# Two buffers for later units' queries, keys and values, six stage tiles, and a plan with other numbers

## The chip, the cores and the metric

The kernel runs on one core of one Trainium2 chip. The metric is device time in microseconds (us) of one launch. Before the change three runs took 918.61, 918.62 and 922.46 us, median 918.62. The engines are named as in the profile: PE is TensorE (matmuls; PEld its weight loads), DVE is VectorE, ACT is ScalarE, POOL is GpSimd, SP is SyncE, which issues all DMAs here, in order.

## What is computed

Windowed attention for 8 batches of 8 heads, 576 positions and 64 columns (heads 4 to 7 look at every fourth position), and then a two-layer network with a rational function between the layers, on 4608 tokens:

```python
scores = scale * np.matmul(q, k.transpose(0, 1, 3, 2))
mask_plain = (rel >= 0) & (rel < 32)
mask_dil = (rel >= 0) & (rel < 128) & (rel % 4 == 0)
attn = softmax(np.where(mask, scores, -1e9))
x = np.matmul(attn, v)          # to (tokens, 512)
h = x @ w_in                    # (4608, 512) x (512, 2048)
P = a[0] + a[1]*h + a[2]*h**2 + a[3]*h**3
Q = 1.0 + abs(b[0])*abs(h) + abs(b[1])*h**2
out = (P / (Q + 1e-6)) @ w_out  # (4608, 2048) x (2048, 512)
```

All is float32. The two large products are each made of three matmuls on a high and a low half of their operands.

## The kernel before

**Units.** The attention is cut into 48 units, six for each batch. A unit loads its queries and keys in one DMA (`qk`, 448 KB) and its values in another (`v`, 384 KB). PE makes its scores, DVE, ACT and POOL the softmax, and PE the product with the values. Units 0 to 5 (batch 0) turn their probabilities on PE. For units 6 to 47 DVE turns them in blocks into a stage tile `u`; a DMA stores that into `turned`, and two DMAs read it back as `pT`. After the values product DVE turns the result into another stage tile `y`, which goes through `results` and comes back as `z` in four DMAs; ACT and DVE or POOL then split `z` into `xh` and `xl`, the high and low half of the input of the network. Six units of a batch fill one chunk of 512 tokens. What of a batch lies beyond 512 tokens is stored to `left` and makes up a ninth chunk.

**Tiles.** The network runs over 144 tiles, one for a chunk and one of 16 column blocks of `w_in`. Tile i has a first product `h` (12 matmuls into one PSUM bank of two), an elementwise chain over DVE, ACT and POOL, and 12 matmuls of the second product into four PSUM banks. The chain ends with a row `a<-a,h` on DVE, which frees the PSUM bank: `h` of tile i + 2 waits for that row of tile i. Tiles 0 to 7 are of chunk 0, tiles 8 to 23 of chunk 1, tiles 24 to 31 the rest of chunk 0, and tiles 32 to 47 of chunk 2. So the first product of tile 8 also needs `xh` and `xl` of units 6 to 11. Chunk 2 takes the `x` slot of chunk 1, so its splits come after tile 23.

**Weights.** 32 weight blocks arrive as 64-bit numbers (512 KB each), and are joined to float32 in a stage tile (`wi_f`, `wo_f` on DVE) and split into two halves on ACT, DVE or POOL, all of it beside the units of chunks 0 and 1 and the first tiles.

**The order.** The class `Plan` writes the order of every engine's instructions before anything is built: a list scheduler with a cost for each operation, a time for each DMA (`DMA_NS`, `DMA_RATE`), a hop between engines, and for each tile pool its number of buffers (`plan.takes`). Among operations that could start, the rank decides, and ranks come from the tables `DUE` (when a batch's units are due, counted in tiles), `LATE` and `SLACK`. The engines then run their rows strictly in that order: a row that waits holds all that stand behind it. SP too issues in order, so a load that waits for its buffer holds the stores and reloads behind it.

`qk` and `v` of units 6 to 47 have one buffer each, in the pool `att`: the load of unit 7's values waits until unit 6's values product is done. The pool tag `stage` has 8 tiles, used in turn for `u`, `y`, `z`, weights in conversion, output copies and others. A unit's values product and the scores of the unit two later are one operation of the plan (`DEPTH`), so in PE's order they stand together.

Of the kernel before, what the change touches and what calls it, by code (L numbers as in the profile page):

```python
# [8 lines left out]
F32 = mybir.dt.float32  # L9
# [10 lines left out]
P = 128  # L20
# [7 lines left out]

START_S, START_O = ["A", "att"] * 3, ["B", "B", "B", "A", "B", "A"]
KIND = [0, 0, 0, 0, 1, 0]  # L30
DUE = [(-23.06, 3.81), (79.36, 5.81), (328.16, 47.85), (161.48, -7.11), (443.73, -17.31), (297.23, -16.95), (114.62, -18.15), (542.56, 10.22)]

LATE = {"ab": -240.26, "ql": -279.92, "pl": -62.25, "qq": -87.68, "t1": 0.97, "t2": -88.2, "ln": 264.97, "ex": -508.74, "g0": -102.98, "g1": -175.35, "g2": -162.43, "gh": -184.66, "gl": 248.86, "out": 3.92}
SLACK = {"sc": 2.61, "qk0": -23.4, "v0": -24.42, "load": -21.21, "wi": 7.7, "wo": -0.04, "w": -8.09, "gl": -0.92, "out": 0.87}

EARLY_TILES, BOTH_TILES = 36, 36

DEPTH, STAGE, AHEAD, ON_PE = 2, 8, 6, 2
LEFT = S - 512
RQ, RKEY, NV = 4 * 3 * 32, 4 * 128, 3 * 2 * 2 * 64  # L40
LOG_SHIFT = 40
# [36 lines left out]
class Plan:  # L78
# [3 lines left out]
    HOP = {"PE": 200.0, "ACT": 135.0, "DVE": 120.0, "POOL": 80.0, "SP": 0.0}  # L82
    MORE = {("PE", "ACT"): 40.0, ("ACT", "POOL"): 110.0, ("DVE", "POOL"): 110.0, ("DVE", "ACT"): 60.0, ("ACT", "DVE"): 15.0}
    DUE_HOP, WINDOW = 150.0, 200.0
    DMA_START, DMA_NS, DMA_RATE = 3300.0, 1600.0, 400.0
    PERIOD, PE_LATE = 4743.0, 105.0

    def __init__(self):
# [2 lines left out]
    def op(self, engs, rank, fn, *deps, dma=0, lock=False):  # L91
        o = Op(engs, rank, fn, deps, dma, lock)
        self.ops.append(o)
        return o
# [88 lines left out]
def tile_attention_moe(  # L183
# [16 lines left out]
    att = ctx.enter_context(tc.tile_pool(name="att", bufs=1))  # L200
# [3 lines left out]
    plan = Plan()  # L204
    op = plan.op
# [50 lines left out]
    class Unit:  # L256
# [4 lines left out]
            self.s, self.o_ps = two_banks(self.s_tag), two_banks(self.o_tag)  # L261

        def load_qk(self, pool, tag):
            t = pool.tile([P, RQ + RKEY], F32, tag=tag, name=f"qk{self.n}")
            load(t, qk[self.n])
            self.q = t[:, :RQ].rearrange("p (g i c) -> p g i c", g=4, i=3)
            self.k = t[:, RQ:].rearrange("p (g k) -> p g k", g=4)

        def load_v(self, pool, tag):
            self.v = pool.tile([P, NV], F32, tag=tag, name=f"v{self.n}")  # L270
            load(self.v, vp[self.n])

        def scores(self):
# [205 lines left out]
        def plan(self, by, tags):  # L479

            b, u, start = self.b, self.u, self.start
            (qp, qt), (vpool, self.vt) = tags if start else ((att, "qk"), (att, "v"))
            self.by = by
            lq = op({"SP": 430}, 0, lambda e: self.load_qk(qp, qt), dma=(RQ + RKEY) * 512)
            self.lv = lv = op({"SP": 430}, 0, lambda e: self.load_v(vpool, self.vt), dma=NV * 512)
            prev, clear = None, []
            masks = [masked, identity] if self.on_pe else []
            if len(Unit.open) >= DEPTH:
                prev = Unit.open.pop(0)
            if prev:  # L490
                sc = op({"PE": 1320 + 300 * self.on_pe}, 0, lambda e: (prev.av(), self.scores()), *prev.placed, prev.lv, lq, *masks)
                clear = prev.finish(sc)
            else:
                sc = op({"PE": 1000 + 300 * self.on_pe}, 0, lambda e: self.scores(), lq, *masks)
            if self.on_pe:
                ma = sc
            else:
                ma = op({"DVE": 400 + 70 * len(MASK_AT[u])}, 0, lambda e: self.mask(), sc, masked)
            if start and KIND[u]:
                mx = op({"DVE": 660}, 0, lambda e: self.max_bank(), ma)  # L500
                su = ex = sm = op({"ACT": 1850}, 0, lambda e: self.exp_bank(), mx)
            else:
                mx = op({"DVE": 470}, 0, lambda e: self.max(), ma)
                su = op({"DVE": 500}, 0, lambda e: self.sub(), mx)
                ex = op({"ACT": 425}, 0, lambda e: self.exp(), su)
                sm = op({"DVE": 470}, 0, lambda e: self.sum(), ex)
            rc = op({"DVE": 300}, 0, lambda e: self.recip(), sm)
            no = op({"POOL": 790}, 0, lambda e: self.norm(e), rc)
            if start:
                tr = op({"PE": 550}, 0, lambda e: self.transposes(), no, identity)  # L510
                pl = op(BOTH, 0, lambda e: self.place(e), tr)
                plan.takes(tr, "h", 2, [pl])
                self.placed = [pl]
            else:
                tr = op({"DVE": 580}, 0, lambda e: self.turn(), no)
                pu = op({"SP": 430}, 0, lambda e: self.put(), tr, dma=P * 384 * 4)
                mv = op({"SP": 900}, 0, lambda e: self.move(), pu, dma=P * 384 * 4 + 160000)
                pu.slack = 0.0
                plan.takes(tr, "stage", STAGE, [pu])
                self.placed = [mv]  # L520


            if not start:
                sc.follows.append(Unit.last_read[0])
            Unit.last_read = [Unit.last_read[1], tr if start else su]
            for o, before in zip((lq, lv, sc), Unit.last):
                if before not in o.follows:
                    o.follows.append(before)
            Unit.last = (lq, lv, sc)
            (first_loads if start else unit_loads).extend((lq, lv))  # L530
            if start:
                early.extend((lq, lv))
            for o in (sc, ma, mx, su, ex, sm, rc, no, tr, *self.placed):
                o.slack = 0.0
            sc.slack = SLACK["sc"]
            lq.slack = SLACK["qk0" if start else "load"]
            lv.slack = SLACK["v0" if start else "load"]
            plan.takes(lq, qt, 1, [sc])
            plan.takes(sc, self.s_tag, 1, [su, *clear])
            plan.takes(su, "p", 2, [tr])  # L540
            plan.takes(mx, "mx", 2, [su])
            plan.takes(sm, "sm", 2, [no])
            if start:
                av = op({"PE": 1000}, 0, lambda e: self.av(), *self.placed, lv)
                av.slack = 0.0
                self.finish(av)
            else:
                Unit.open.append(self)

        def finish(self, av):  # L550
            b, start = self.b, self.start
            main, left = self.pieces()
            got = av
            if not start:
                to = op({"DVE": 590}, 0, lambda e: self.turn_out(), av)
                po = op({"SP": 430}, 0, lambda e: self.put_out(), to, dma=P * 384 * 4)
                got = op({"SP": 1800}, 0, lambda e: self.move_out(), po, dma=P * 384 * 4 + 160000)
                to.slack = po.slack = got.slack = 0.0
                plan.takes(to, "stage", STAGE, [po])
            eh = op({"ACT": sum(172 + 2 * c[1] / 1.4 * 0.75 for c, _ in main)}, 0, lambda e: self.evac_hi(), got)  # L560
            low = {"DVE": sum(120 + 2 * c[1] / 0.96 for c, _ in (main + left if start else main))}
            if not start:
                low["POOL"] = sum(100 + 2 * c[1] / 0.49 for c, _ in main)
            el = op(low, 0, lambda e: self.evac_lo(e), eh, lock=not start)
            eh.slack = el.slack = 0.0
            el.by = self.by
            lf = None
            if left:
                lf = op({"SP": 430 * len(left)}, self.by + 2.0, lambda e: self.put_left(), el if start else got, dma=P * 2 * LEFT * 4 + 60000)
                left_done.append(lf)  # L570
                if start:
                    plan.takes(el, "stage", STAGE, [lf])
            if start:
                plan.takes(self.placed[0], "a", 2, [av])
                plan.takes(av, self.o_tag, 1, [el])
            else:
                plan.takes(got, "stage", STAGE, [x for x in (el, lf) if x])
                plan.takes(self.placed[0], *(("p", 2) if self.n % 2 else ("pT", 1)), [av])
            plan.takes(self.lv, self.vt, 1, [av])
            if b not in x_done:  # L580
                x_done[b] = []
                plan.takes(eh, "x" + x_slot(b), 1, h_done[b])
            else:
                eh.deps.append(x_done[b][0])
            x_done[b] += [eh, el]
            return [el] if start else [to]
# [267 lines left out]
    identity = op({"POOL": 1000}, -89, lambda e: make_idents())  # L854
# [13 lines left out]
    for b in range(1, B):  # L868
        last, step = DUE[b]
        for u in range(NU):  # L870
# [124 lines left out]
```

## Time and profile before

| | |
|---|---|
| three runs, median | 918.62 us |
| the profiled execution | 921.15 us |
| its span, first to last instruction | 919.4 us |
| mean granted clock of PE | 0.989 |
| DMA | 105.81 MB, 115 GB/s over the span |
| most DMA issues | qk x48 (448 KB), v x48 (384 KB), weights x32 (512 KB), pT x84 (96 KB) |

The span's slices on the page give each engine's busy share, PE's granted clock and the DMA engines' share. Idle time of an engine counts only where it holds the chain that ends last; on the page 67% of that chain is PE's. The critical rows are shown where the prediction uses them.

### The profile page before, as it was taken

Reading aid. Unit: us, or ns where it says so; the run is one execution under the profiler, and the core shown is the slowest. Engines: PE = TensorE matmul, PEld = TensorE weight load, DVE = VectorE, ACT = ScalarE, POOL = GpSimd, SP = SyncE. Lnnn points to the kernel's source line nnn. Section 1 sums busy time; section 2 is a strip of 40 time slices with the busy share of each in tenths; the row PEclk is TensorE's granted clock in tenths of the full one; section 3 lists DMA queues with packets and bytes.
Section 4 is the critical chain, followed back from the end, with each engine's and each line's share of the span. In section 5 each row is a group of like instructions: output and inputs, shape, how many; then the busy total and the mean of one; then the engine's idle time right before and its main releaser. Section 6 shows DMA issues by size and latency. Waiting matters only on the chain.

```text
span 919.4 us, 21111 instructions
## 1 busy us (share of the span) xinstructions
PE 880.5 (96%) x8106; PEld 712.5 (77%) x8106; DVE 744.3 (81%) x1322; ACT 677.9 (74%) x1082; POOL 482.9 (53%) x419
## 2 busy tenths in 40 slices
PE   6858899999999999999999999999999999999998
PEld 4646688777888888788878888887888878888876
DVE  4787898999988988888879878987879777657656
ACT  3666899777767877777777777767777688777764
POOL 2456657475545664456455555545455444544442
PEclk9979999999999999999999999999999999999999
DMA  9668543335553343434343334422233220001001
GB/s 343 202 216 267 181 149 115 129 102 176 165 176 103 111 142 116 129 100 128 90 155 112 102 92 145 148 65 83 100 121 98 77 69 1 1 0 47 1 1 46
DMA packets 90372, 105.81 MB, mean 115 GB/s; under 512 B 40736, under 2 KB 67744, under 8 KB 90272
## 3 DMA queue, kind: packets, MB, share of 16 engines
q1 hardware_dynamic: 90272, 104.47, 35.6%
q8 instruction: 63, 1.03, 0.5%
q14 instruction: 37, 0.30, 0.1%
HBM read 76.39 MB, written 28.05 MB: 114 GB/s over the span
## 4 chain that ended last, share of the span: by engine, by line
PE 67%; DVE 11%; DMA 7%; ACT 7%; issue 3%; POOL 3%; SPq 2%; POOLq 0%; ACTq 0%; DVEq 0%
PE h L211 30%; PE out L211 30%; PE pair L211 4%; ACT r L214 4%; DVE a L220 3%; DVE h L220 3%; SPq L208 2%; POOL a L223 2%; DMA results<-y 2%; DMA turned<-u 1%; DMA qk<-in_qk_dram 1%; DMA z<-results 1%; DVE t L217 1%; DMA v<-in_vp_dram 1%; DMA wi_raw<-in_w_in_dram 1%
## 5 line engine op out<-in xcount | busy, mean ns | idle before, releaser
L211 PE MATMUL h<-xh,wi 128*128 128x512 f32 x1136 | 379.6, 396 | 10.3 <-DVE a L220 10.1
L211 PE MATMUL out<-gh,wo 128*128 128x512 f32 x1136 | 355.5, 394 | 0.0
L223 POOL TENSOR_TENSOR a<-r,a 128x512 f32<-128x512 f32 x126 | 163.1, 1295 | 256.0 <-ACT r L214 241.1
L211 PEld LDWEIGHTS h<-xh,wi 128*128 128x128 f32 x1136 | 215.9, 190 | 63.1 <-DVE a L220 17.4
L211 PEld LDWEIGHTS out<-gh,wo 128*128 128x128 f32 x1136 | 211.4, 189 | 45.7
L223 POOL TENSOR_TENSOR gl<-a,gh 128x512 fp32r<-128x512 f32 x135 | 186.8, 1383 | 72.0 <-ACT gh L214 56.4
L211 PE MATMUL h<-xl,wi 128*128 128x512 f32 x568 | 223.6, 394 | 0.0
L211 PE MATMUL out<-gl,wo 128*128 128x512 f32 x568 | 221.9, 391 | 0.9 <-DVE gl L217 0.9
L220 DVE SCALAR_TENSOR_TENSOR a<-a,r 128x512 f32<-128x512 f32 x141 | 100.2, 710 | 100.5 <-ACT r L214 98.7
L214 ACT ACTIVATE r<-a,ln_bias 128x512 f32<-128x512 f32 x141 | 101.8, 722 | 90.9 <-POOL a L223 87.3
L214 ACT ACTIVATE r<-a,ab_t 128x512 f32<-128x512 f32 x141 | 115.0, 815 | 15.0 <-DVE a L220 6.4
L211 PEld LDWEIGHTS out<-gl,wo 128*128 128x128 f32 x568 | 107.0, 188 | 24.0 <-DVE gl L217 1.3
L211 PEld LDWEIGHTS h<-xl,wi 128*128 128x128 f32 x568 | 108.0, 190 | 21.7
L214 ACT ACTIVATE t<-h,na_t 128x512 f32<-128x512 f32 x142 | 109.6, 772 | 11.5 <-PE h L211 11.5
L214 ACT ACTIVATE a<-h 128x512 f32<-128x512 f32 x140 | 83.4, 596 | 41.4 <-PE h L211 37.8
L220 DVE SCALAR_TENSOR_TENSOR h<-h,na_t,r 128x512 f32<-128x512 f32 x142 | 106.6, 751 | 7.0 <-ACT r L214 6.1
L220 DVE SCALAR_TENSOR_TENSOR h<-t,na_t,h 128x512 f32<-128x512 f32 x142 | 107.2, 755 | 4.8
L214 ACT ACTIVATE r<-r,exp_bias 128x512 f32<-128x512 f32 x144 | 104.3, 724 | 4.6
L217 DVE TENSOR_TENSOR t<-t,h 128x512 f32<-128x512 f32 x142 | 96.3, 678 | 11.2 <-ACT t L214 8.9
L220 DVE SCALAR_TENSOR_TENSOR a<-a,h 128x512 f32<-128x512 f32 x140 | 96.2, 687 | 4.6
L214 ACT ACTIVATE gh<-a 128x512 fp32r<-128x512 f32 x133 | 83.4, 627 | 18.9 <-PE out L211 14.7
L223 POOL TENSOR_TENSOR p<-p,sm 128x384 f32<-128x384 f32 x48 | 45.3, 945 | 39.8 <-DVE sm L342 35.1
(105 smaller groups left out, 691.4 us busy)
## 6 DMA issues: line engine op xcount, KB each, us to landing
qk<-in_qk_dram SPq DMA_DIRECT2D x48, 448.0 KB, 4.8
v<-in_vp_dram SPq DMA_DIRECT2D x48, 384.0 KB, 3.9
out_dram<-os SPq DMA_DIRECT2D x36, 256.0 KB, 2.3
wi_raw<-in_w_in_dram SPq DMA_DIRECT2D x16, 512.0 KB, 5.3
wo_raw<-in_w_out_dram SPq DMA_DIRECT2D x16, 512.0 KB, 6.2
turned<-u SPq DMA_DIRECT2D x42, 192.0 KB, 2.2
pT<-turned SPq DMA_DIRECT2D x84, 96.0 KB, 2.5
results<-y SPq DMA_DIRECT2D x42, 192.0 KB, 2.5
```

The lines of the kernel that those rows point to most:

```text
L208: pin(nc.sync.dma_start(dst, src))
L211: pin(nc.tensor.matmul(o, lhs, rhs, start=start, stop=stop))
L214: pin(nc.scalar.activation(o, i, func, **kw))
L217: pin(nc.vector.tensor_tensor(o, x, y, op))
L220: pin(nc.vector.scalar_tensor_tensor(o, x, s, y, op0, op1))
L223: pin(nc.gpsimd.tensor_tensor(o, x, y, op))
```

## The change

It gives `qk` and `v` of units 6 to 47 two buffers each, cuts the stage tiles from 8 to 6, gives the leftover stores a rank 20 tiles after their unit's due time instead of 2, and changes numbers that only the planner reads: the tables of due times and ranks, a DMA's time and rate, and the PE times of units 0 to 11. No instruction's arithmetic changes.

```diff
-DUE = [(-23.06, 3.81), (79.36, 5.81), ...
-LATE = {"ab": -240.26, "ql": -279.92, ...
-SLACK = {"sc": 2.61, "qk0": -23.4, "v0": -24.42, "load": -21.21, ...
+DUE = [(-24.06, 4.46), (-57.85, 3.6), ...
+LATE = {"ab": -115.18, "ql": -320.79, ...
+SLACK = {"sc": 1.84, "qk0": -29.55, "v0": -32.24, "load": 0.45, ...
...
-DEPTH, STAGE, AHEAD, ON_PE = 2, 8, 6, 2
+DEPTH, LOADS, STAGE, AHEAD, ON_PE = 2, 2, 6, 6, 2
...
-    DMA_START, DMA_NS, DMA_RATE = 3300.0, 1600.0, 400.0
+    DMA_START, DMA_NS, DMA_RATE = 3300.0, 1750.0, 375.0
...
-            t = pool.tile([P, RQ + RKEY], F32, tag=tag, name=f"qk{self.n}")
+            t = pool.tile([P, RQ + RKEY], F32, tag=tag, name=f"qk{self.n}", bufs=LOADS if pool is att else 1)
...
-            self.v = pool.tile([P, NV], F32, tag=tag, name=f"v{self.n}")
+            self.v = pool.tile([P, NV], F32, tag=tag, name=f"v{self.n}", bufs=LOADS if pool is att else 1)
...
-                sc = op({"PE": 1000 + 300 * self.on_pe}, 0, lambda e: self.scores(), lq, *masks)
+                sc = op({"PE": 1130 + 320 * self.on_pe}, 0, lambda e: self.scores(), lq, *masks)
...
-                tr = op({"PE": 550}, 0, lambda e: self.transposes(), no, identity)
+                tr = op({"PE": 690}, 0, lambda e: self.transposes(), no, identity)
...
-            plan.takes(lq, qt, 1, [sc])
+            plan.takes(lq, qt, 1 if start else LOADS, [sc])
...
-                av = op({"PE": 1000}, 0, lambda e: self.av(), *self.placed, lv)
+                av = op({"PE": 1500}, 0, lambda e: self.av(), *self.placed, lv)
...
-                lf = op({"SP": 430 * len(left)}, self.by + 2.0, lambda e: self.put_left(), ...
+                lf = op({"SP": 430 * len(left)}, self.by + 20.0, lambda e: self.put_left(), ...
...
-            plan.takes(self.lv, self.vt, 1, [av])
+            plan.takes(self.lv, self.vt, 1 if start else LOADS, [av])
```

Since ranks and times move, so does the order on every engine. Three places show it. The first is SP's queue in the start part; the number in a name is the unit or the weight block (`left_80<-l2` is unit 2's leftover). Before:

```order
L208 DMA v5_141<-in_vp_dram 128x768
L208 DMA wi_raw2_169<-in_w_in_dram 128x512
L208 DMA wi_raw3_171<-in_w_in_dram 128x512
L208 DMA qk6_173<-in_qk_dram 128x896
L208 DMA v6_201<-in_vp_dram 128x768
L208 DMA left_80<-l2_473 128x2x64
L208 DMA wi_raw4_517<-in_w_in_dram 128x512
L208 DMA left_80<-l3_550 128x2x16
L208 DMA qk7_587<-in_qk_dram 128x896
```

And now:

```order
L208 DMA qk6_171<-in_qk_dram 128x896
L208 DMA v5_173<-in_vp_dram 128x768
L208 DMA qk7_175<-in_qk_dram 128x896
L208 DMA v6_203<-in_vp_dram 128x768
L208 DMA v7_207<-in_vp_dram 128x768
L208 DMA left_80<-l2_508 128x2x64
L208 DMA wi_raw4_526<-in_w_in_dram 128x512
L208 DMA left_80<-l3_559 128x2x16
L208 DMA qk8_594<-in_qk_dram 128x896
```

Unit 7's loads now stand ahead of the first leftover store; before, its values stood behind the reload of its own `pT`, 17 rows behind that store.

The second place is PE where units 7 to 9 meet tile 2: `pair<-v7,pT7` is unit 7's values product, `pair<-qk9` unit 9's scores, `h2` the first product of tile 2. Before:

```order
L211 MATMUL pair_85<-v7_826,pT7_763 32x64 x24
L211 LDWEIGHTS ident_b_91
L211 MATMUL pair_85<-mask_t_89,ident_b_91 128x192
L211 LDWEIGHTS ident_b_91
L211 MATMUL pair_85<-mask_t_89,ident_b_91 128x192
L211 MATMUL pair_85<-qk9_833 32x64 x24
L211 MATMUL h2_947<-xh0_318,wi2_672 128x512
```

And now:

```order
L211 MATMUL pair_85<-qk9_682 32x64 x24
L211 MATMUL pair_85<-v8_827,pT8_957 32x64 x24
L211 LDWEIGHTS ident_b_91
L211 MATMUL pair_85<-mask_t_89,ident_b_91 128x192
L211 LDWEIGHTS ident_b_91
L211 MATMUL pair_85<-mask_t_89,ident_b_91 128x192
L211 MATMUL pair_85<-qk10_830 32x64 x24
L211 MATMUL h2_1048<-xh0_325,wi2_609 128x512
```

Unit 8's values product and unit 10's scores moved ahead of `h2`; in exchange `h1`, which stood ahead of unit 6's values product, now stands behind unit 8's scores.

The third place is DVE just ahead of the first product of tile 8. In a name the number after `a`, `h`, `t` or `r` is the tile, that after `xl1<-z` the unit. Before:

```order
L217 TENSOR_TENSOR t7_1587<-t7_1587,h7_1554 128x512
L220 SCALAR_TENSOR_TENSOR h7_1554<-t7_1587,na_t_96,h7_1554 128x512
L220 SCALAR_TENSOR_TENSOR a6_1533<-a6_1533,r6_1551 128x512
L220 SCALAR_TENSOR_TENSOR a6_1533<-a6_1533,h6_1491 128x512
L220 SCALAR_TENSOR_TENSOR wo_f7_1509<-wo_f7_1509,wo_raw7_1402 128x512
L217 TENSOR_TENSOR a7_1594<-r7_1624,a7_1594 128x512
```

And now:

```order
L220 SCALAR_TENSOR_TENSOR wi_f9_1540<-wi_f9_1540,wi_raw9_1282 128x512
L217 TENSOR_TENSOR wo7_1593<-wo_f7_1523,wo7_1593 128x512
L226 CAST wi9_1606<-wi_f9_1540 128x512
L220 SCALAR_TENSOR_TENSOR h6_1439<-h6_1439,na_t_96,r6_1574 128x512
L341 TENSOR_SCALAR sm12_1569<-sm12_1569 128x3x2
L342 RECIPROCAL sm12_1569<-sm12_1569 128x6
L311 TENSOR_REDUCE mx13_1617<-pair_85 128x6
L217 TENSOR_TENSOR p13_1624<-pair_85,mx13_1617 128x384
L220 SCALAR_TENSOR_TENSOR a6_1528<-a6_1528,r6_1574 128x512
L220 SCALAR_TENSOR_TENSOR a6_1528<-a6_1528,h6_1439 128x512
L217 TENSOR_TENSOR xl1_974<-z11_1598,xh1_973 128x2x32
L217 TENSOR_TENSOR xl1_974<-z11_1598,xh1_973 128x256
```

The last row on DVE that tile 8 needs was `a6<-a6,h6`, the 161st on DVE, with unit 11's `xl` on POOL; now it is unit 11's `xl`, the 174th, and rows of weight blocks 7 and 9 and of unit 13 stand ahead of it.

More of the change, by code (lines that the diff above doesn't have):

```diff
@@ L30 @@
 KIND = [0, 0, 0, 0, 1, 0]
-DUE = [(-23.06, 3.81), (79.36, 5.81), (328.16, 47.85), (161.48, -7.11), (443.73, -17.31), (297.23, -16.95), (114.62, -18.15), (542.56, 10.22)]
-LATE = {"ab": -240.26, "ql": -279.92, "pl": -62.25, "qq": -87.68, "t1": 0.97, "t2": -88.2, "ln": 264.97, "ex": -508.74, "g0": -102.98, "g1": -175.35, "g2": -162.43, "gh": -184.66, "gl": 248.86, "out": 3.92}
-SLACK = {"sc": 2.61, "qk0": -23.4, "v0": -24.42, "load": -21.21, "wi": 7.7, "wo": -0.04, "w": -8.09, "gl": -0.92, "out": 0.87}
+DUE = [(-24.06, 4.46), (-57.85, 3.6), (402.88, 53.88), (116.9, 16.69), (421.9, -10.28), (292.95, -31.74), (99.19, -14.28), (576.86, 35.06)]
+LATE = {"ab": -115.18, "ql": -320.79, "pl": -155.39, "qq": -213.84, "t1": 4.81, "t2": -32.02, "ln": 215.19, "ex": -546.51, "g0": -99.62, "g1": -305.02, "g2": -315.69, "gh": -180.38, "gl": 259.95, "out": 3.96}
+SLACK = {"sc": 1.84, "qk0": -29.55, "v0": -32.24, "load": 0.45, "wi": 12.67, "wo": 1.65, "w": -17.63, "gl": -1.67, "out": -1.52}
 EARLY_TILES, BOTH_TILES = 36, 36
-DEPTH, STAGE, AHEAD, ON_PE = 2, 8, 6, 2
+DEPTH, LOADS, STAGE, AHEAD, ON_PE = 2, 2, 6, 6, 2
 LEFT = S - 512
@@ L568, in finish @@
             if left:
-                lf = op({"SP": 430 * len(left)}, self.by + 2.0, lambda e: self.put_left(), el if start else got, dma=P * 2 * LEFT * 4 + 60000)
+                lf = op({"SP": 430 * len(left)}, self.by + 20.0, lambda e: self.put_left(), el if start else got, dma=P * 2 * LEFT * 4 + 60000)
                 left_done.append(lf)
```

## The prediction

> **What bounds the kernel now.** First the page's busy times, for how full the engines are.
> ```profile
> PE 880.5 (96%) x8106; PEld 712.5 (77%) x8106; DVE 744.3 (81%) x1322; ACT 677.9 (74%) x1082; POOL 482.9 (53%) x419
> ```
> TensorE (PE) is busy for 96% of the span, so at most some 39 us of idle time can go. The table of busy time by stretch (start:end, length, busy of each engine, granted clock, DMA share, GB/s) says where it lies.
> ```profile
> 0.00:25.00 25.00, 16.28 (x459) 12.29 (x459) 12.79 (x36) 8.27 (x26) 7.28 (x19) 1.00 0.87 328
> 25.00:110.00 85.00, 64.90 (x1003) 49.93 (x1004) 68.63 (x140) 60.88 (x108) 51.21 (x49) 0.90 0.72 224
> 110.00:256.00 146.00, 142.19 (x1154) 115.07 (x1155) 136.49 (x230) 118.23 (x193) 87.06 (x76) 0.99 0.43 140
> 256.00:900.00 644.00, 641.57 (x5428) 522.62 (x5427) 514.57 (x901) 482.54 (x747) 333.49 (x274) 1.00 0.29 88
> ```
> After 256 us PE idles 2.4 us in 644: nothing to win there. From 25 to 110 us it idles 20.1 us, at a mean clock of 0.90, and from 110 to 256 it idles 3.8 us while VectorE (DVE) is busy for 136.49 of 146. So the change is decided before 256 us. What PE waits for between 35 and 110 us is the next view (total, times, longest).
> ```profile
> PE pair L211 <- DMA v<-in_vp_dram: 10.7, 2, 8.3
> PE h L211 <- DVE a L220: 5.5, 4, 1.9
> ```
> Two waits for a unit's values make up most of it. On PE's timeline they stand before the values products of units 7 and 9; the other rows are h2 (the first product of tile 2), the values products of units 8 and 11, and h8.
> ```profile
> 53.30 0.96 PE L211 MATMUL pair<-v,pT 64*32 64x64 f32 x48 [8.27 <-DMA v<-in_vp_dram]
> ...
> 57.43 0.79 PE L211 MATMUL h<-xh,wi 128*128 128x512 f32 x1 [1.84 <-DVE a L220]
> ...
> 62.85 0.77 PE L211 MATMUL pair<-v,pT 64*32 64x64 f32 x48
> ...
> 74.64 0.71 PE L211 MATMUL pair<-v,pT 64*32 64x64 f32 x48 [2.47 <-DMA v<-in_vp_dram]
> ...
> 91.84 0.80 PE L211 MATMUL pair<-v,pT 64*32 64x64 f32 x44 [0.36 <-DVE wo_f L220]
> ...
> 109.84 0.50 PE L211 MATMUL h<-xh,wi 128*128 128x512 f32 x1 [1.90 <-DVE a L220]
> ```
> h8, at 109.84 us, opens the part in which PE hardly pauses; I call its start T8. Both orders put the same PE work before it: the first products of tiles 0 to 7, 72 matmuls of second products, the scores up to unit 13, the values products up to unit 11. So T8 can be compared directly.
>
> **The change, part by part.** With two buffers the loads of unit 7's keys and values leave SyncE (SP) ahead of the first leftover store. Before, SP stood waiting for the copies of those stores (first row, DVE's l), and it issued unit 7's values at 45.41 us only, when unit 6 had freed the one buffer:
> ```profile
> SPq L208 <- DVE l L226: 12.6, 4, 7.2
> ```
> ```profile
> 43.91 1.41 SPq L208 DMA_DIRECT2D pT<-turned  x2
> 45.41 0.69 SPq L208 DMA_DIRECT2D v<-in_vp_dram  x1
> ```
> What is late next at 53.30 us? The DMAs issued from 43.5 to 45.4 us and from 45.4 to 46 us (KB each, us to landing) say it:
> ```profile
> pT<-turned SPq DMA_DIRECT2D x2, 96.0 KB, 8.1
> v<-in_vp_dram SPq DMA_DIRECT2D x1, 384.0 KB, 7.8
> ```
> Unit 7's turned probabilities (pT), started at 43.91 and some 0.6 later, landed at 52.0 to 52.6, just before the values at 45.41 + 7.8 = 53.2. SP had issued four weight tiles directly ahead of them, and still does. So of the 8.27 us the buffers alone remove 0.6 to 1.3. The 2.47 us can go whole, but the new order runs unit 8's values product directly after unit 9's scores, with h2 behind it. Unit 8's chain then holds PE: from its scores over softmax, store and reload to its pT, issued at 56.94 and 2.7 to landing, at 59.6 to 60.2.
> ```profile
> 44.31 0.72 PE L211 MATMUL pair<-qk 64*32 64x64 f32 x48
> ```
> ```profile
> 56.94 1.24 SPq L208 DMA_DIRECT2D pT<-turned  x2
> ```
> ```profile
> pT<-turned SPq DMA_DIRECT2D x2, 96.0 KB, 2.7
> ```
> Between unit 8's scores (44.31) and its values product both orders hold equal PE work (one values product, one set of scores, one first product), so no PE time is won here, only the 1 us or so by which the chain starts sooner. A wait of over 5 us stays, and with it the slow clock: from h2's start at 57.43 to the next row's 62.85 its twelve matmuls took 5.4 us.
> The Trainium skill ("TensorE: Matmul & The Clock Gate", Part 1) says that an idle window of about 3.4 us drops the clock to half, and that as long of sustained work restores it. Priced by that rule each such wait costs about 1.7 us more (an estimate from the page), and if one more of them arose than there is now, the sum below would be 1.7 us higher. The 5.4 us of h2 agree with half a clock.
>
> What then sets T8 is DVE. Up to the last DVE row that h8 needs, the new order has 13 rows more: 174 against 161. Five a<-r,a, three more joined weights, three more low halves of weights and six xl pieces come over from GpSimd (POOL) or from later; casts, copies and rows of tile 7 leave. Two of the kinds, with their mean ns:
> ```profile
> L217 DVE TENSOR_TENSOR a<-r,a 128x512 f32<-128x512 f32 x15 | 12.0, 799 | 3.3 <-ACT r L214 3.2
> ...
> L217 DVE TENSOR_TENSOR xl<-pair_B,xh 128x384 fp32r<-128x384 f32 x2 | 1.1, 554 | 2.3 <-ACT xh L214 2.3
> ```
> 13 rows at 0.55 to 0.80 are 7.2 to 10.4 us; as most of the xl pieces are short I take 8. From 25 us on DVE then needs 68.6 + 8 = 76.6 us before T8, and its idle time. That was 85 - 68.6 = 16.4 us, of which:
> ```profile
> DVE mx L311 <- PE pair L211: 4.1, 5, 1.4
> DVE t L217 <- ACT t L214: 2.3, 2, 1.7
> DVE t L217 <- ACT a L214: 2.0, 2, 1.6
> ```
> The 4.1 us for scores that stood behind late values should go, and the added rows fill the 4.3 us in which DVE waited for ScalarE (ACT): 16.4 - 4.1 - 4.3 = 8.0. **T8 = 25 + 76.6 + 8.0 = 109.6**, 0.2 us sooner. With an idle time between 0 and 16.4 it is 101.6 to 118.0.
>
> Next, h8 to h24, where PE and DVE run neck and neck:
> ```profile
> 125.00:200.00 75.00, 72.22 (x495) 58.21 (x494) 71.12 (x111) 63.82 (x103) 43.89 (x37) 1.00 0.37 129
> ```
> ```profile
> 114.45 2.76 PE out L211 x12
> 117.22 2.72 PE h L211 x12
> ```
> ```profile
> 160.66 0.67 PE L211 MATMUL pair<-v,pT 64*32 64x64 f32 x44
> ...
> 161.79 0.50 PE L211 MATMUL h<-xh,wi 128*128 128x512 f32 x1
> ...
> 206.63 0.39 PE L211 MATMUL h<-xh,wi 128*128 128x512 f32 x1
> ```
> A DVE row takes 71.12 / 111 = 0.64 us, at 95% use. Eight tiles of PE take 8 x 2 x 2.72 = 43.5 us, and a values product with the next scores 1.2 (160.66 to 161.79). DVE rows between the last products of tiles 6, 14 and 22: before 64 and 76, after 72 and 73. Before: 64 x 0.64 / 0.95 = 43.1, under PE's 43.5; then 51.2, over PE's 47.1 with three pairs; sum 94.7, and with 1.8 of slow clock after T8 96.5, where the trace has 206.63 - 109.84 = 96.8. After: 48.5 and 49.2, sum 97.7, the slow clock beneath it. That is **1.2 later** (0.9 to 3.0, with and without that cover). But by h32 the new order has one more pair done, work that is not to come: **-1.2**.
>
> At nothing I cost: eight stage tiles made six (units' results of chunk 2 stay in them until tile 23; what hides it is that the units behind have over 17 us of PE work before their values products; uncovered, about one tile, 5.4 us); six output copies that go from DVE to ACT after tile 47, where DVE is busy for 514.57 of 644 us; the leftover stores' later rank and the planner's numbers in themselves; the tail, whose last 60 rows on DVE and POOL stand as before. Unit 6's turn on DVE stands two rows earlier in the start part, the 1 us above; it is in T8.
> **Sum: -0.2 + 1.2 - 1.2 = -0.2 us.** The profiled execution took 921.15 us, its span of 919.4 and 1.75 around it; that is 2.5 over the median of 918.62, inside the runs' 918.61 to 922.46. The sum gives 920.95 for it and 918.4 for the median.
>
> **Rivals.**
> - *The stalls go.* Loads now run at 25 to 40 us, into a DMA share of 0.72, so unit 7's pT may land sooner as well, and DVE's idle time fall to 2 us: T8 = 103.6, 6.2 sooner, 912.4. For it: 10.7 us of waits for v. Against: that pT landed with the values, and unit 8's chain.
> - *DVE's longer list is paid in full* (the slower side). Place: the DVE rows ahead of h8. If the 16.4 us of idle time stay, T8 = 118.0, 8.2 later: 926.8. Beyond 8.2 us of idle time it is slower than before, beyond 12.8 by over 0.5%. For it: from unit 11's values product to h8 the new order has 9.5 us of PE work (before 13.6), while that chain took 18.0 us (91.84 to 109.84).
> - *Early loads push the small transfers back.* pT took 8.1 us behind four weights and 2.7 behind little. A pair of loads (832 KB, 2.3 us at the 362 GB/s below) now stands ahead of unit 8's pT and one ahead of unit 11's results: 4.6 us, 923.0.
> ```profile
> 44.00:48.00 4.00, 1.03 (x60) 0.68 (x50) 3.23 (x7) 2.50 (x5) 1.95 (x3) 1.00 0.99 362
> ```
> The Trainium skill ("DMA: Bandwidth & Descriptors", Queues, rings and completion order) says that each DMA engine takes descriptors in ring order, which speaks against issuing loads early; the 8.1 us agree.
> - *Nothing changes*: the loads of units 8 and 9 still wait on SP for the products of units 6 and 7. 918.6.
>
> **How the numbers follow.** My forecast 0.38 (own range 914 to 923; same 0.34, faster 0.02, slower 0.02); stalls go 0.37 (faster 0.34, same 0.03); longer list 0.15 (slower 0.13, same 0.02); pushed back 0.06 (half same, half slower); nothing 0.04. Together: faster by over 0.5% (below 914.0) 0.36, same 0.46, slower (above 923.2) 0.18; 0.5% is about what a measurement of this kernel can tell from no change. Range: 909 (idle time near 0 and little slow clock) to 926 (most of the longer list).
>
> **What would show it.** Right: T8 at 107 to 112 us, PE waiting over 4 us for unit 8's pT before h2, no wait for v, and PE's waits of 110 to 256 us on DVE. For the first rival: T8 below 105, unit 7's pT landing before 50 us. For the second: DVE idle for over 14 us between 25 us and T8. For the third: results and pT over 5 us to landing. Waits of PE after 256 us would make the whole account wrong.

## The result, and the profile after

The changed kernel took **922.08 us** (median of 20 runs, 918.81 to 926.46) against 919.10 for before (20 runs, 915.60 to 922.46): ratio 1.0038, 95% interval 1.0024 to 1.0052. So it is 3 us slower, where the forecast was 0.2 us faster: inside the range, but not by the forecast's account. The profiled execution took 924.11 us, its span 922.3. Three executions of later runs, one each of e5, e6 and e7, took 1243.92 to 1726.88 us, far above all others, and no median below counts them.

The page's busy times, and the stretches of the table shown before (start:end, length, busy of PE, PEld, DVE, ACT, POOL, clock, DMA share, GB/s):

```profile
PE 877.3 (95%) x8106; PEld 708.4 (77%) x8106; DVE 735.6 (80%) x1321; ACT 684.8 (74%) x1090; POOL 467.1 (51%) x412
```
```profile
25.00:110.00 85.00, 61.52 (x969) 46.20 (x969) 71.82 (x146) 59.48 (x104) 39.16 (x37) 0.80 0.75 240
110.00:256.00 146.00, 143.04 (x1254) 115.29 (x1253) 133.11 (x236) 117.26 (x192) 81.70 (x73) 1.00 0.44 140
256.00:900.00 644.00, 640.80 (x5332) 522.06 (x5332) 505.14 (x889) 486.77 (x751) 332.46 (x280) 1.00 0.27 86
```

From 25 to 110 us PE does 3.4 us less and idles 23.5 us instead of 20.1. DVE does 3.2 more there, POOL 12 less. PE's waits between 35 and 110 us (total, times, longest), then five rows of its timeline: the values products of units 7 (begun at 52.49, the rest at 53.15), 8 and 11, h7 and h8:

```profile
PE pair L211 <- DMA pT<-turned: 9.6, 4, 8.6
PE pair L211 <- DVE wi_f L220: 5.5, 1, 5.5
PE h L211 <- DVE a L220: 3.5, 2, 3.2
```
```profile
52.49 0.39 PE L211 MATMUL pair<-v,pT 64*32 64x64 f32 x2 [5.47 <-DVE wi_f L220]
53.15 0.95 PE L211 MATMUL pair<-v,pT 64*32 64x64 f32 x46 [0.27 <-DMA pT<-turned]
...
64.00 1.48 PE L211 MATMUL pair<-v,pT 64*32 64x64 f32 x48 [8.57 <-DMA pT<-turned]
...
98.36 0.67 PE L211 MATMUL pair<-v,pT 64*32 64x64 f32 x44 [0.59 <-DVE p L217]
...
105.73 0.50 PE L211 MATMUL h<-xh,wi 128*128 128x512 f32 x1 [3.23 <-DVE a L220]
...
113.03 0.50 PE L211 MATMUL h<-xh,wi 128*128 128x512 f32 x1
```

The waits for v are gone, as foretold. In their place PE waits 5.7 us before unit 7's product and 8.57 before unit 8's, and T8 is 113.03 instead of 109.84.

**Where the 3 us are.** One profile is one execution, and those of a kernel spread over some 7 us. So each kernel was profiled a second time (e6, e12 below). The rows are the stretches from 25 us to T8, from T8 to the start of h25, and from there to h50; first before and its second profile, then after and its second profile:

```profile
25.00:109.84 84.84, 64.75 (x1002) 49.77 (x1002) 68.47 (x140) 60.72 (x108) 51.05 (x49) 0.90 0.72 225
109.84:214.76 104.92, 101.11 (x792) 81.40 (x793) 98.79 (x158) 89.09 (x144) 64.72 (x54) 0.98 0.39 129
214.76:361.80 147.04, 147.04 (x1549) 119.83 (x1548) 131.19 (x246) 108.78 (x173) 79.93 (x73) 1.00 0.44 134
```
```profile
25.00:107.65 82.65, 64.52 (x1002) 49.44 (x995) 68.28 (x139) 60.09 (x108) 50.20 (x49) 0.81 0.73 230
107.65:211.99 104.34, 101.07 (x793) 81.38 (x794) 98.44 (x158) 89.40 (x144) 64.87 (x54) 0.98 0.38 130
```
```profile
25.00:113.03 88.03, 64.55 (x981) 48.40 (x980) 74.70 (x152) 62.14 (x110) 40.87 (x38) 0.81 0.73 234
113.03:213.39 100.36, 97.52 (x697) 79.29 (x697) 92.94 (x157) 84.48 (x137) 59.79 (x51) 1.00 0.35 118
213.39:362.52 149.13, 147.48 (x1453) 118.57 (x1452) 127.99 (x236) 108.75 (x176) 75.95 (x71) 1.00 0.42 129
```
```profile
25.00:112.38 87.38, 65.61 (x1051) 50.22 (x1035) 74.45 (x160) 63.28 (x115) 41.19 (x39) 0.88 0.75 236
112.38:212.45 100.07, 97.52 (x697) 79.15 (x697) 93.36 (x157) 84.49 (x136) 58.48 (x51) 1.00 0.36 118
```

Between two such marks the two orders do the same PE work, but for pairs of units' operations at 1.2 us: the new order has one fewer done by h25, two fewer by h50, none by the last tile. The means of the two profiles, with this taken out:

| stretch | before | after | after - before | without the pairs |
|---|---|---|---|---|
| start to T8 | 108.75 | 112.71 | +4.0 | +4.0 |
| T8 to h25 | 104.63 | 100.22 | -4.4 | -3.2 |
| h25 to h50 | 147.10 | 148.72 | +1.6 | +2.8 |
| h50 to h143 | 539.93 | 541.54 | +1.6 | -0.8 |
| h143 to the end | 17.56 | 18.37 | +0.8 | +0.8 |

They add up to 3.6, while the medians differ by 3.0. No stretch alone is the loss: most of the start's is paid back behind T8, and another is made behind h25. What is paid back is for the most part PE's clock, as the rows from h8 to h24 show further down.

### The profile page after: what moved, and what is told of

The parts are those of the page before. It is cut to its first block, busy times and chain, and to the rows that moved or that the text cites. A ratio compares the mean times of both kernels' runs of the same rounds, so it can differ in the third digit from the quotient of the medians.

```text
span 922.3 us, 21079 instructions
## 1 busy us (share of the span) xinstructions
PE 877.3 (95%) x8106; PEld 708.4 (77%) x8106; DVE 735.6 (80%) x1321; ACT 684.8 (74%) x1090; POOL 467.1 (51%) x412
## 4 chain that ended last, share of the span: by engine, by line
PE 61%; DVE 12%; ACT 4%; DMA 4%; issue 2%; POOL 2%; SPq 2%; DVEq 0%; POOLq 0%; ACTq 0%
PE h L211 29%; PE out L211 29%; DVE a L220 3%; PE pair L211 3%; ACT r L214 3%; DVE h L220 3%; SPq L208 2%; DMA results<-y 2%; DMA z<-results 1%; POOL a L223 1%; DVE t L217 1%; DVE xl L217 1%; DMA wo_raw<-in_w_out_dram 1%; DVE y L399 1%; ACT t L214 1%
## 5 line engine op out<-in xcount | busy, mean ns | idle before, releaser
L223 POOL TENSOR_TENSOR a<-r,a 128x512 f32<-128x512 f32 x129 | 167.1, 1296 | 290.3 <-ACT r L214 280.2
L223 POOL TENSOR_TENSOR gl<-a,gh 128x512 fp32r<-128x512 f32 x134 | 180.0, 1343 | 58.7 <-ACT gh L214 41.6
L214 ACT ACTIVATE gh<-a 128x512 fp32r<-128x512 f32 x137 | 85.9, 627 | 16.7 <-PE out L211 10.2
```

The lines of the kernel that those rows point to most:

```text
L214: pin(nc.scalar.activation(o, i, func, **kw))
L223: pin(nc.gpsimd.tensor_tensor(o, x, y, op))
```

## The experiments

**Tool.** The planner answers any edit with a new order everywhere. So in most kernels its answer was written out as a table of operations with their engines and replayed; an edit then moves the named rows and no other. "Old order" and "new order" are those of before and after.

```diff
     def run(self):
...
+        name = {"P": "PE", "A": "ACT", "D": "DVE", "G": "POOL", "S": "SP"}
+        for x in ORDER.split():
+            self.ops[int(x[:-1])].fn(name[x[-1]])
```

**e6, e12: both kernels again.** Nothing but the table.

> The changed kernel once more, with its own order written out (every engine's instructions as in after): a second profile, to tell what belongs to the kernel from what belongs to one execution. Time 921 to 923, ratio 1.0024 to 1.0052. If the new order itself makes the later start and the losses between tiles 25 and 50, T8 is 111.5 to 114.5 again and 4.5 to 5.2 us are lost between tiles 25 and 50 (before 1.8); if they are chance, T8 falls to 110 and the loss below 3.

> The kernel before once more, its own order written out, for a second profile: T8 within 1.5 us of 109.84, 1.5 to 2.2 us lost between tiles 25 and 50, time 916 to 922. If T8 comes out below 108, the first profile of before was a late one, by as much as its time (921.15) stood over the median.

e6 took 922.23 us (ratio 1.0036, 1.0024 to 1.0049), T8 at 112.38. e12 took 918.33 in its one run, T8 at 107.65. So the later start belongs to the new order, and the profile that the prediction was worked from was one with a late start, by 2.2 us. From h25 to h50 PE idles 1.7 and 1.5 us in the new order, and not at all in the old (length less busy time in the rows above; e12 as before).

**e1, e2: which half of the order?** The table of one kernel up to h25, then what is left in the order of the other, with two buffers and six tiles.

> The order is written out as a table: the order of before up to the plan's start of tile 25's first product, then what is left in the order of after; two buffers for keys and values and six stage tiles throughout (so a dozen rows stand a little later than in before). Theory S (the loss is made in the start part, before tile 8, and carried to the end): T8 at 109 to 111, time 918 to 920, ratio to before 0.999 to 1.001. Theory L (the later start is made good by tile 25, where the table of lost time has both kernels level, and the new order loses 2 to 3 us behind it): 921 to 923, ratio 1.002 to 1.004.

> The reverse: the order of after up to tile 25's first product, then what is left in the order of before. Theory S: T8 at 112 to 114, time 921 to 923, ratio 1.002 to 1.004. Theory L: T8 at 112 to 114 as well, but time 918 to 920, ratio 0.999 to 1.001. Should both e1 and e2 come out at 922 or both at 919, neither part alone is the cause.

e2 took 924.62 us (1.0048, 1.0027 to 1.0069): the new start with the old rest is no faster than the new order, so theory L falls. It does not show theory S whole: T8 is 111.40, where S had 112 to 114, the time lies above its 921 to 923, and e2's stretch from h25 to h50 took 149.19 us, 2.1 more than the old order's 147.10 for the same PE work. e1 can't be read: 931.44 us (1.0125, 1.0096 to 1.0155), T8 at 116.53. Its old half stood in six tiles, which is dear by itself, as e5 shows.

**e3, e4, e5, e11, e15, e16: the parts of the change.** e5 and e3 are the old order with six tiles, and with two buffers and early unit loads as well; e4 is the new order with one buffer, e11 that with eight tiles, e15 the planner with buffers and tiles new and all its numbers old, e16 the changed kernel with the old rank of the leftovers.

```diff
-DEPTH, LOADS, STAGE, AHEAD, ON_PE = 2, 2, 6, 6, 2
+DEPTH, LOADS, STAGE, AHEAD, ON_PE = 2, 1, 6, 6, 2
...
-                lf = op({"SP": 430 * len(left)}, self.by + 20.0, lambda e: self.put_left(), ...
+                lf = op({"SP": 430 * len(left)}, self.by + 2.0, lambda e: self.put_left(), ...
```

(The first pair is e4, the second e16.)

> The buffers alone: the order of before on PE, DVE, ACT and POOL (six stage tiles, so a dozen rows a little later), two buffers for keys and values, and only SP's loads of units' keys and values moved up to where the second buffer allows them. Theory X (early loads take the place of weights on the way in, ScalarE stands for weights, and that is the loss): ScalarE waits for wi_raw over 4 us between 25 and 70 us (before 0.6), T8 at 111 to 114, time 920 to 923. Theory Y (the order does it, the buffers are worth a little): the wait of 8.27 us before unit 7's values product shrinks by 0.6 to 1.3 and the 2.47 us one goes, T8 at 108 to 110, time 917 to 919.

> The buffers undone in the new order: one buffer each again, every other instruction of every engine in the order of after, and SP's unit loads as late as one buffer makes them. Theory X: ScalarE's waits for wi_raw fall from 8.3 to below 3 us, T8 1 to 3 us sooner than 113, time 919 to 921. Theory Y: the waits for v come back on PE, T8 at 114 to 120, time 922 to 928.

> Six stage tiles alone: the order of before written out, one buffer each for keys and values, six stage tiles in place of eight (a dozen rows stand later where the planner's order asks for a seventh tile). The prediction costed this at nothing. Theory P (that is right, and e3's 23 us came from its early loads): 918 to 921, ratio 0.999 to 1.002. Theory T (the old order lives on its eight tiles, and e3 lost its 23 us for want of them): 930 to 945, PE waiting over 4 us for results (y) that wait for a stage tile, as in e3.

> e4 (the order of after, one buffer each for keys and values, SP's unit loads late) with eight stage tiles in place of six: the price of six tiles in the new order. If six tiles cost it nothing, as forecast: 931.5 to 934 as e4, and 4.5 to 5.2 us lost between tiles 25 and 50. If the tiles make the losses between tiles 25 and 50: these fall to 2 us, time 929 to 931. If they make the start's: T8 below 121 (e4: 123.78).

> Two buffers and six stage tiles with every number of the planner as before (its tables, transfer and TensorE times, the rank of the leftover stores): what the buffers bring when the planner may use them, and nothing is tuned to them. If the new tables are what makes six tiles bearable, this is slow: 928 to 945 (the old order in six tiles took 936). If the buffers and tiles are neutral in themselves: 917 to 923.

> The changed kernel with the leftover stores' rank as before (2 in place of 20 behind the unit's due time). Forecast: nothing, 921 to 923, T8 at 111.5 to 114. If the later leftovers had cost something: below 920; if they had saved SP's stand before unit 8's transfers: above 924.

| | us | ratio to before, 95% | T8 |
|---|---|---|---|
| e5 old order, six tiles (three runs) | 933.69 | 1.0169 (1.0134 to 1.0203) | - |
| e3 the same, two buffers, early loads | 942.19 | 1.0240 (1.0210 to 1.0269) | 109.66 |
| e15 two buffers, six tiles, old numbers | 940.85 | 1.0232 (1.0195 to 1.0269) | 116.55 |
| e4 new order, one buffer | 932.63 | 1.0136 (1.0110 to 1.0161) | 123.78 |
| e11 the same, eight tiles | 932.35 | 1.0137 (1.0106 to 1.0169) | 125.41 |
| e16 new order, early leftovers | 922.42 | 1.0033 (1.0017 to 1.0049) | 111.49 |

Six tiles, with the rows that have to stand later for them, cost the old order some 15 us. The new order with one buffer loses nothing by them (e11 against e4). Early loads brought the old order no sooner T8, and some 7 us more in all (e3 against e5). The new order lives on its second buffers: without them PE waits 18.0 us for pT (9.6 in after), though SP's loads are all that was moved. The row is PE's wait up to T8 in e4:

```profile
PE pair L211 <- DMA pT<-turned: 18.0, 4, 8.0
```

So buffers and tiles with the old numbers cost 22 us (e15), and the new numbers get 19 of them back. e5's loss was not traced. The leftovers' rank is worth nothing that the runs can tell (e16).

**e9, e10, e18: are the stalls worth anything?** The old order with eight tiles, and one after the other what PE waited for between 44 and 57 us taken away: unit 7's (and 9's) values by places of their own, then unit 7's pT by a reload ahead of the four weights, then unit 9's keys.

```diff
     def load_v(self, pool, tag):
+            pool, tag = {7: (wpool, "wi9"), 9: (wpool, "wo9")}.get(self.n, (pool, tag))
...
     def load_qk(self, pool, tag):
+            pool, tag = {9: (wpool, "wi8")}.get(self.n, (pool, tag))
```

> The stalls for values alone, taken out of the old order: before with its order written out and its eight stage tiles; the values of units 7 and 9 get places of their own (in tiles that hold weights only after 90 us), unit 7's load is issued right behind unit 6's and unit 9's behind unit 8's; no other row moves. Forecast's step: the 8.27 us wait shrinks by 0.6 to 1.3 only, since pT lands as late, the 2.47 us wait goes whole, T8 at 108 to 110, time 917 to 919.5. Rival (the stalls go): T8 below 105, time 912 to 914. Rival C (VectorE's list sets h2 and T8 whatever PE waits for before): T8 109 to 110, time 918.5 to 920.

> e9, and on SP the reload of unit 7's pT ahead of the four weight tiles that stood before it (wi7, wo0 to wo2). If pT behind the weights was what kept the 8.27 us, it lands at 46 to 48 us, the wait before unit 7's values product falls below 2.5 us, and PE waits for h2 instead, on tile 0's last a row (57.43 in before): T8 107 to 110. Time 916 to 919 if T8 is carried; 918.5 to 921 by rival C, or if the later weights cost ScalarE and VectorE what PE gains.

> e10, and the keys of unit 9 too in a place of their own, loaded behind unit 8's: the last of the three things that one after the other held PE between 44 and 57 us in the old order (unit 7's values, its pT, unit 9's keys). If PE's stalls were worth their length: the wait of 6.08 us before unit 9's scores goes, T8 falls below 106, time below 916. Rival C (VectorE's list sets h2, h3 and T8 whatever PE waits for before): PE waits as long for tile 0's last a row instead, h2 at 55 to 58, T8 at 107 to 110, time 918 to 920.5.

PE's rows in e9 (unit 7's values product), in e10 (the same, and unit 9's scores) and in e18 (the same product, then h2):

```profile
51.93 1.10 PE L211 MATMUL pair<-v,pT 64*32 64x64 f32 x48 [6.00 <-DMA pT<-turned]
```
```profile
47.64 0.88 PE L211 MATMUL pair<-v,pT 64*32 64x64 f32 x48 [3.03 <-DVE y L400]
55.02 0.97 PE L211 MATMUL pair<-qk 64*32 64x64 f32 x48 [6.08 <-DMA qk<-in_qk_dram]
```
```profile
48.71 0.97 PE L211 MATMUL pair<-v,pT 64*32 64x64 f32 x48 [2.46 <-DVE y L401]
59.57 0.80 PE L211 MATMUL h<-xh,wi 128*128 128x512 f32 x1 [8.56 <-DVE a L220]
```

Each time the next thing is late: pT, then the keys, and at last VectorE's row a of tile 0, for which h2 waits 8.56 us. T8 stood at 108.14, 109.68 and 108.82, and the times were 919.22, 920.21 and 920.10 us, ratios 0.9996 (0.9981 to 1.0012), 1.0003 (0.9986 to 1.0020) and 1.0007 (0.9991 to 1.0022). So the stalls that the change removes were worth nothing, within some 2 us: they stood in front of VectorE's list.

**e7, e8, e17: single rows of the new order.** e7 puts h2 ahead of unit 8's product and the copies of z6 behind rows of tiles 0 and 1; e8 also puts unit 8's pT first on SP and its exp on ACT; e17 puts unit 11's chain ahead, with its product behind h5, and the softmax of unit 13 further back. The moves in PE's queue (e7, then e17):

```
+h2 x12
 pair<-v8,pT8  pair<-qk10
-h2 x12
...
 h5 x12
+pair<-v11,pT11  pair<-qk13
 out x12, h6 x12
-pair<-v11,pT11  pair<-qk13
```

> The new order with three rows moved: on PE h2 ahead of the operation that holds unit 8's values product and unit 10's scores; on ScalarE and VectorE the copies of unit 6's results (xh, xl from z) behind the rows of tiles 0 and 1 that h2 and h3 wait for. Theory Z (z6, landing at 63.4 us, stands ahead of tile 0's last a row on VectorE's list, and unit 8's chain ahead of h2 on PE's; that makes the late T8, and T8 is carried to the end): h2 starts at 61 to 64 (66.7 in after), T8 at 109 to 111.5, time 919 to 921. Rival C (VectorE's list until tile 25 sets the end, whatever T8): T8 comes sooner, the time stays at 921 to 923.

> e7, and in addition unit 8's chain put first: on SP its pT reload ahead of the loads of unit 11's keys and of z6, on ScalarE its exp ahead of the weights of tile 7. Theory Z: unit 8's pT lands at 60 to 62 (63.9 in after), T8 at 107 to 110, time 916 to 920. Rival C: T8 sooner, time 920 to 923.

> The new order with unit 11's chain put ahead: its turned probabilities earlier on VectorE and SP, its pT reload ahead of the loads of units 12 and 14, unit 12's mask, max and subtraction ahead (they hold the scores' bank), and the operation of unit 11's values product and unit 13's scores right behind h5 in place of behind h6. In the chain of waits of the changed kernel tile 8 stands for unit 11's results (values product at 98.36 to 98.88, T8 some 13.5 to 14.7 later), in that of before for VectorE. Theory U (that is the late T8): the values product at 91 to 95, T8 at 107 to 109.5, time 917.5 to 920. Rival V (VectorE's rows ahead of T8 would have been as late): the values product at 91 to 95, T8 at 111 to 114, time 921 to 923.5.

h2 and h8 in e7; in e17 unit 11's product, h7 and h8:

```profile
64.83 0.79 PE L211 MATMUL h<-xh,wi 128*128 128x512 f32 x1 [8.25 <-DVE a L220]
...
115.05 0.50 PE L211 MATMUL h<-xh,wi 128*128 128x512 f32 x1
```
```profile
93.40 0.67 PE L211 MATMUL pair<-v,pT 64*32 64x64 f32 x44 [2.21 <-DVE y L399]
...
105.72 0.50 PE L211 MATMUL h<-xh,wi 128*128 128x512 f32 x1 [2.73 <-DVE a L220]
...
112.90 0.39 PE L211 MATMUL h<-xh,wi 128*128 128x512 f32 x1
```

Theories Z and U fall. With h2 ahead, the 8.57 us for pT became 8.25 us for row a of tile 0, h2 came 1.9 us sooner and T8 2 us later. With unit 11's product 5 us sooner, h7 stood at the same 105.72, waiting for row a of tile 5. e8, with unit 8's chain first, had h2 at 63.94 (after 7.40 us for the same row a) and T8 at 115.92. Times of e7, e8 and e17: 923.20 us (1.0038, 1.0021 to 1.0055), 924.30 (1.0055, 1.0033 to 1.0076) and 925.92 (1.0071, 1.0053 to 1.0090).

**e13: VectorE's longer list.** Eleven rows ahead of T8 back on GpSimd, such as these:

```
-DVE L217 a1<-r1,a1   (also tiles 3, 4, 5, 6)
+POOL L223 a1<-r1,a1
-DVE L217 xl<-z6,xh   (also units 8, 9, 11)
+POOL L223 xl<-z6,xh
```

> The new order with eleven rows ahead of T8 given back to GpSimd, where the old order had them (five a<-r,a of tiles 1, 3, 4, 5, 6, the low halves xl of units 6, 8, 9, 11, two low halves of weights); nothing else moves. Theory M (the later T8 is VectorE's longer list: 74.2 to 75.5 us of work from 25 us to T8 in six profiles of the new order, 67.9 to 68.5 in four of the old): VectorE's work falls to 67.5 to 69.5, T8 comes at 107.5 to 110.5, time 918 to 920.5. Rival G (GpSimd's 1.3 us for a row that took VectorE 0.7 stands on the tiles' chain as well): VectorE's idle time grows by what its work falls, T8 stays at 112 to 115, time 921.5 to 925.

The stretch to T8 in e13, then one group of DVE's rows in that stretch, of after and of e13 (count | busy, mean ns | idle before):

```profile
25.00:112.15 87.15, 63.41 (x984) 48.65 (x981) 72.64 (x143) 62.68 (x113) 53.45 (x50) 0.88 0.75 240
```
```profile
L220 DVE SCALAR_TENSOR_TENSOR a<-a,r 128x512 f32<-128x512 f32 x7 | 5.5, 779 | 0.0
L220 DVE SCALAR_TENSOR_TENSOR h<-t,na_t,h 128x512 f32<-128x512 f32 x7 | 5.2, 748 | 0.1
```
```profile
L220 DVE SCALAR_TENSOR_TENSOR a<-a,r 128x512 f32<-128x512 f32 x7 | 7.0, 1000 | 0.0
L220 DVE SCALAR_TENSOR_TENSOR h<-t,na_t,h 128x512 f32<-128x512 f32 x7 | 5.2, 747 | 0.1
```

Rival G, for the most part: 921.55 us (1.0020, 1.0005 to 1.0034), T8 at 112.15. Eleven rows fewer, some 7 us at their durations in after (five a<-r,a at 687 ns, four xl at 340 to 557, two low halves of weights), took only 1.9 us off DVE's work (72.64 us, after 74.70 and 74.45). With GpSimd busier (53.45 us instead of 40.87) DVE's large groups on two SBUF tiles grew (a<-a,r 779 to 1000 ns, and 740 in e6; wi_f 847 to 952, wo_f 762 to 921), while those that also read PSUM did not (748, 747); and DVE idled 14.5 us instead of 13.1. The Trainium skill ("GPSIMD Engine Reference", Specifications) says that GpSimd shares its SBUF interfaces with VectorE, in contention with DVE instructions on two SBUF inputs; these two groups agree.

**e14: a version that beats both.** The old order, eight tiles, one buffer, with six rows behind T8 given to GpSimd: a<-r,a of tiles 14 to 19.

```
-DVE L217 a14<-r14,a14   (also tiles 15 to 19)
+POOL L223 a14<-r14,a14
```

> A version that might beat both: the old order, eight tiles, with the a<-r,a of tiles 14 to 19 on GpSimd in place of VectorE, in the stretch where the old order loses most behind T8 (5.3 to 5.9 us between tiles 18 and 25, VectorE busy 40.96 of 42 us from 165 to 207). If VectorE's list is the bound there, six rows of 0.65 us less give 2 to 4 us: time 915.5 to 917.5. If the longer GpSimd rows stand on the chain: 919 to 921.

The stretch from T8 to h25 in e14:

```profile
108.89:210.04 101.15, 100.42 (x792) 81.27 (x793) 92.03 (x151) 88.61 (x143) 71.46 (x59) 0.98 0.39 132
```

It took **916.59 us**, ratio 0.9969 (0.9952 to 0.9986). The stretch is 3.2 us shorter than in the second profile of before (104.34), with DVE at 92.03 instead of 98.44 us. PE idles 0.7 us there, where it idled 3.8 and 3.3. So in the old order VectorE's list held PE up behind T8, and six rows less on it move the end.

## Why the prediction was wrong

The forecast's terms against the two profiles of each order:

| term | forecast | before, e12 | after, e6 | difference of the means |
|---|---|---|---|---|
| T8 | -0.2 | 109.84, 107.65 | 113.03, 112.38 | +4.0 |
| h8 to h24 | +1.2 | 96.78, 96.78 | 94.92, 94.64 | -2.0 |
| h24 to h32 | 0 | 48.92, 48.38 | 50.34, 49.58 | +1.3 |
| h32 to the end | -1.2 | 663.82, 663.74 | 663.99, 664.17 | +0.3 |

No term came out. That the sum missed by only some 3 us is luck: the misses have both signs.

- **T8, its idle time (the step that failed).** The sum took DVE's work to T8 as 76.6 us and its idle time as 8.0, because waits for late scores "should go" and the added rows would fill others. The work was 74.7 and 74.5, the idle time 13.3 and 12.9: it hardly shrank (16.4 and 14.4 in before). The two kinds of wait did shrink, those for scores from 4.1 us to 2.0, those for ACT's t and a from 4.3 to none. But others grew in their place, as these rows of DVE's waits up to T8 show (after, then before; in e6 4.1 us for xh, 2.5 for p and 1.6 for GpSimd's p):

```profile
DVE sm L338 <- ACT p L214: 5.3, 4, 1.8
DVE xl L217 <- ACT xh L214: 3.9, 3, 2.0
DVE mx L311 <- PE pair L211: 2.0, 2, 1.1
```
```profile
DVE xl L217 <- ACT xh L214: 1.9, 3, 0.9
DVE sm L338 <- ACT p L214: 1.2, 1, 1.2
```

  That VectorE sets T8 fits: from 103.78 us on it does not pause, and its row a6 ends at 112.98, where h8 begins at 113.03. So 6.2 us more work (8 forecast) cost 4 us. Taking PE's stalls away one by one left DVE's idle time at 15.0, 16.8 and 16.2 in e9, e10 and e18. Rival 2 fits best, at half its price (its sign, over 14 us of idle time, is just missed), but no run shows the longer list alone as the cause: e13 took 1.9 us of the work back, the idle time grew by 1.4, and T8 came 0.6 sooner. Which rows would have to move for the idle time to go stays open; it is 11 to 17 us in every profile but those of e1, e4, e11 (22 to 25) and e5. e17 and e7 only show that it isn't unit 11's chain, nor h2's place.
- **T8 as a lever.** The waits for v were read as PE time to be won, or as moved to pT. The second is right for unit 7 (8.27 us became 5.7; forecast 7.0 to 7.7), and unit 8's product held PE 8.57 us (over 5 forecast; its pT came at 64.0, not at 60). But e9, e10 and e18 show no price of such waits in the old order, and e7 and e8 none of the new one before unit 8's product.
- **h8 to h24.** +1.2 was forecast, from 145 rows of DVE at the price of 0.64 us each and 95% use; measured is -2.0. The stretch in before, then in after:

```profile
109.84:206.63 96.79, 94.01 (x673) 75.83 (x673) 90.83 (x143) 82.64 (x133) 59.48 (x49) 0.98 0.36 123
```
```profile
113.03:207.95 94.92, 92.08 (x673) 74.79 (x673) 87.53 (x147) 80.02 (x130) 57.89 (x49) 1.00 0.36 121
```

  DVE did run four rows more, but shorter ones, 0.60 us each, and had slack (87.5 us of 94.9). PE ran the same matmuls with the same idle time (2.8 us in both); only its busy time fell, by 1.9 us, with a granted clock of 1.00 instead of 0.98. This is the slow stretch that the forecast priced at 1.8 us and left beneath DVE's rows. In before and e12 it stands at h8, whose twelve matmuls took 4.45 us (h9: 2.72). In after and e6 it stands at h7 (4.45 and 4.20), ahead of T8 and beside a VectorE that does not pause.
- **One more pair by h32, -1.2**: the count is right, but the sum is not. The pair is done between h24 and h32 and costs its time there (+1.3), which the sum left out, and from h32 on nothing was won (+0.3).
- **Nothing behind 256 us**: wrong. From h25 to h50 the new order loses 2.8 us more. DVE's groups there (before, then after) and a wait of ACT in after:

```profile
L220 DVE SCALAR_TENSOR_TENSOR h<-h,na_t,r 128x512 f32<-128x512 f32 x25 | 18.8, 750 | 0.8 <-ACT r L214 0.4
```
```profile
L220 DVE SCALAR_TENSOR_TENSOR h<-h,na_t,r 128x512 f32<-128x512 f32 x25 | 18.9, 754 | 5.4 <-ACT r L214 5.4
```
```profile
ACT r L214 <- DVE h L220: 4.3, 9, 1.5
```

  DVE waits 5 us more for ACT's r, and ACT 4.3 us for DVE's h, which frees the one r tile. No run changed these rows alone, so this is a reading, not shown. The new order's buffers and tiles are not it: the stretch takes 148.98 us in e4 and 148.85 in e11. And in e2, whose rest is the old order, ACT waits only 0.5 us for DVE's h, and 2.1 us are lost all the same.
- **Costed at nothing**: the leftovers' rank (e16) is right, and so are six tiles in the new order, as far as one buffer tells (e11 against e4). Uncovered, in the old order, six tiles cost some 15 us (e5), not the 5.4 that was named.
- **Rivals.** "The stalls go" falls with e18. "Early loads push back" has something in the old order (e3). In after its sign is there, results and pT over 5 us to landing (7.8 and 8.3), but it is in before as well (7.4 and 8.1), and the new order with late loads has T8 later still (e4). "Nothing changes" is out: the waits for v did go.
- **The base.** The working stood on one profile, whose T8 was 2.2 us later than the next one's. That is as much as the effect looked for.

## What to carry to other kernels

A wait on the fullest engine has a price only if nothing as late stands behind it: look up the row that comes next and what releases it, before a stall is counted as a gain. Where one engine's list is the bound, the same holds for its own waits: keep its idle time as measured, unless a run shows that it goes. Work that is done earlier must be paid for in the stretch where it is now done, and rows are priced by their kinds, not by a mean. An order written out as a table makes single edits of a planned kernel testable; six rows moved off the bound engine did more here than buffers, tiles and every table.

## What the runs showed of the hardware

- Rows given to GpSimd make VectorE's rows on two SBUF tiles longer: 779 (740 in e6) to 1000 ns for a<-a,r in e13, so that eleven rows fewer saved 1.9 us and not 7.
- Two profiles of one order differed in T8 by up to 2.2 us (109.84, 107.65), and from there on ran nearly alike (104.92 and 104.34 us to h25). In before 2.2 of the 2.8 us between the two spans (919.4, 916.5) are made ahead of T8, in the new order 0.7 of 1.5.
- Behind a wait of 1.9 us h8's twelve matmuls took 4.45 us in before, e12, e9 and e14, and 2.86 and 2.85 in e10 and e18, behind a wait as long. A slow stretch cost 1.7 us, and whether it came did not follow from the length of the wait alone.
